# Fourteen matmuls with an unread result between the output projection's matmuls

## The chip, the cores and the metric

One core of a Trainium2 chip runs the kernel. The metric is the device time of one execution in microseconds (us); less is better. The number compared is the median of the runs shown. The engines are TensorE (PE in the profile, with its weight loads as PEld), VectorE (DVE), ScalarE (ACT), GpSimd (POOL) and SyncE (SP), which here issues most of the transfers.

## The reference

A gated sum of an attention decode step and a small MLP, for 8 batch rows with one token each. The keys and values used are the last 1024 positions of caches of 4096.

```python
x = A_x                                        # 8, 1, 448
g = sigmoid((x * gate_w).sum(-1, keepdims=True))
# attention: 16 query heads, 8 kv heads, head size 256, window W = 1024
q = (x @ wq) in heads
scores = einsum("bhqd,bhkd->bhqk", q, k[last W]) * 256 ** -0.5
o = einsum("bhqk,bhkd->bhqd", softmax(scores), v[last W])
a = o.reshape(8, 1, 4096) @ wo                 # 4096 x 448
# MLP
h = gelu(layernorm(x) @ w1 + b1)               # 1792 wide
b = h @ w2 + b2
return g * a + (1 - g) * b
```

## The kernel before

All 77.7 MB of inputs go through a ring of four large SBUF slots, in one order written out by hand: keys and values batch by batch, then the MLP weights (w12), the last values ("v", 7), and at the end the output weights wo. SyncE issues these loads; a slot is filled again when its reader has said done(). For each batch the kernel transposes keys, forms scores in the PSUM tile S_ps, takes the softmax, and multiplies by the values; the softmax and value steps of a batch lie between the key transposes of the next. The instruction order on each engine is the order of the program, since the schedule is manual.

After the last batch come the MLP's hidden layer (mlp_hidden, which gives hs) and the last values (L504, into PO, then oP). The output stage follows, from L628. It multiplies 46 chunks of 128 rows with their weights: 14 chunks of hs with w2, then 32 chunks of oP with wo, which are numbered 0 to 31 here. The first 34 of the 46 are wide: L640 adds each over 448 columns into one of four groups of 32 PSUM partitions of A1, so that four matmuls that follow each other use different columns of the PE array. VectorE then adds the four groups' tile and b2s into accs (L647). The last 12 chunks, 20 to 31, are narrow: L656 splits each into two halves of 224 columns, which go to the tiles A2[0] or A2[1] by the list part; accs itself is brought in by a matmul with pick at place EARLY = 4 among them, after chunk 23. When the last matmul into A2[1] is through, VectorE copies that tile to early (L664); after the last into A2[0] it adds both into res (L665), and two DMAs write res out (L667).

The output weights come in seven transfers (cuts, L166): chunks 0 to 7, 8 to 15, 16 to 19, 20 to 23, 24 and 25, 26 to 29, 30 and 31. TensorE waits for a transfer where it first needs one of its chunks. S_ps, the scores' tile, is last read by the exponential of batch 7 (L450); the identity tile ident is made at the start; the last value tile lies in its slot to the end.

Of the kernel before, what the change touches and what calls it, by code (L numbers as in the profile page):

```python
# [17 lines left out]
def kernel(  # L18
# [15 lines left out]
    nc = tc.nc  # L34
    P = nc.NUM_PARTITIONS

    NB, Sq, D = A_x.shape
    _, Hkv, Sk, Dh = A_k_cache.shape
# [16 lines left out]
    FB = FQ // BL  # L55
    HH = HD // 2
    FH = F // 2
    QN = 512
# [11 lines left out]
    TAIL = 12  # L70
    EARLY = 4
    DOUBLE = (4,)
    qscale = float(Dh) ** -0.5

    xf = A_x.rearrange("b s d -> (b s) d")
# [34 lines left out]
    def slot(*key):  # L110
        return slots[index[key]]
# [80 lines left out]
    ident = consts.tile([P, P], BF16)  # L192
# [4 lines left out]
    S_ps = ps_s.tile([P, W], F32)  # L197
# [149 lines left out]
    def transpose_keys(b, between=None):  # L347
        between = between or {}
        kn = slot("k", b)[:].bitcast(F32)
        for hh in range(NG):  # L350
            kt = ktpool.tile([P, QD, NCK, SK, NJ], BF16, tag="kt", name="kt")
            KT[hh] = kt
            for i in range(NCK // CB):
                g = hh * (NCK // CB) + i
                n = 2 if b in DOUBLE else 1
                if g < n:
# [278 lines left out]
        (hs[:, c, :], w2[:, OW2 + c * D : OW2 + (c + 1) * D]) for c in range(FB)  # L635
    ] + [(oP[:, c % J8, c // J8, :], w[:, c * D : (c + 1) * D]) for c in range(NCH)]
    wide, narrow = chunks[:-TAIL], chunks[-TAIL:]
    for i, (lhsT, rhs) in enumerate(wide):
        g = i % QD
        nc.tensor.matmul(  # L640
            A1[BL * g : BL * g + NB, :],
            lhsT=lhsT,
            rhs=rhs,
            start=(i < QD),
            stop=(i >= len(wide) - QD),
        )
    nc.vector.tensor_tensor(accs[:], A1[:], b2s[:], op=ALU.add)  # L647
    narrow.insert(EARLY, (pick[:], accs[:]))
    part = [1, 0, 1, 0, 0, 1, 1, 1, 0, 1, 0, 0, 0]
# [2 lines left out]
    for i, (lhsT, rhs) in enumerate(narrow):  # L652
        k = part[i]
        for h in range(2):
            g = 2 * k + h
            nc.tensor.matmul(  # L656
                A2[k][BL * g : BL * g + NB, :],
                lhsT=lhsT,
                rhs=rhs[:, h * DO : (h + 1) * DO],
                start=(k not in part[:i]),  # L660
                stop=(k not in part[i + 1 :]),
            )
        if 1 not in part[i + 1 :] and k == 1:
            nc.vector.tensor_copy(early[:], A2[1][2 * BL : P, :])  # L664
    nc.vector.tensor_tensor(res[:], A2[0][0 : 2 * BL, :], early[:], op=ALU.add)  # L665
# [32 lines left out]
```

## Time and profile before

| what | value |
|---|---|
| median of 3 runs | 190.55 us (190.50 to 190.69) |
| span of the profiled execution, first to last instruction | 188.9 us |
| PE busy / PEld busy | 118.8 us / 76.7 us |
| DVE / ACT / POOL busy | 111.7 / 90.6 / 59.0 us |
| mean granted TensorE clock | 0.876 |
| read from HBM | 77.67 MB, 411 GB/s over the span |
| last L504 matmuls start | 173.03 us |
| output stage's first matmul, L640 | 176.89 us |
| final addition L665 | 186.07 to 186.45 us |
| output DMAs issued, L667 | 186.48 us |

The page gives no total time for the profiled execution beside its span; the median of the runs is 1.65 us above that span. The granted clock is the share of full speed that the throttle allowed TensorE: 1.00 is full, 0.50 is half. A transfer's landing is seen as the moment at which an engine that waited for it goes on. Busy time of a matmul in the profile reaches to its modelled end, so it includes the time in which the result drains while the next matmul already streams.

### The profile page before, as it was taken

The page shows a single profiled execution, that of the slowest core. Times are in us where ns is not written, and L with a number is a line of the kernel's source. Part 1 is how long each engine was busy: PE and PEld are TensorE (multiplying, and loading weights), DVE is VectorE, ACT ScalarE, POOL GpSimd, SP SyncE. Part 2 cuts the span into 40 slices and gives each one's busy share as a digit, 9 for nine tenths or more (in the row PEclk, how much of TensorE's full clock was granted, in tenths as well). Part 3 has the DMA queues.
Part 4 walks back from the last instruction along what each step waited for, and adds up shares of the span by engine and source line. Part 5 has one row for each costly group of instructions (what it writes and reads, how often), then busy time and mean ns, then how long its engine had stood idle before and what let it go on. Part 6 is the DMA issues. An engine that isn't in the chain of part 4 may idle for free.

```text
span 188.9 us, 2891 instructions
## 1 busy us (share of the span) xinstructions
PE 118.8 (63%) x1100; PEld 76.7 (41%) x1100; DVE 111.7 (59%) x250; ACT 90.6 (48%) x102; POOL 59.0 (31%) x143
## 2 busy tenths in 40 slices
PE   0678609779775478846767478448853885273453
PEld 0656205555652176415642455147623772010110
DVE  4283783964789548716893487119821784947511
ACT  2298610894993239624762396218931884001000
POOL 8580000670670058003980391029201930000000
PEclk9996975999999969997899999858999799968555
DMA  5999999999999999999999999999999999999990
GB/s 203 418 427 425 451 420 425 434 437 427 420 435 431 434 423 430 428 437 430 420 437 434 434 420 430 437 423 432 423 437 427 434 423 424 418 425 438 413 389 34
DMA packets 7273, 77.86 MB, mean 412 GB/s; under 512 B 846, under 2 KB 1244, under 8 KB 2012
## 3 DMA queue, kind: packets, MB, share of 16 engines
q1 hardware_dynamic: 7226, 77.67, 96.9%
q8 instruction: 8, 0.13, 0.3%
q14 instruction: 5, 0.04, 0.1%
q10 hardware_dynamic: 34, 0.01, 0.0%
HBM read 77.67 MB, written 0.01 MB: 411 GB/s over the span
## 4 chain that ended last, share of the span: by engine, by line
DMA 75%; PE 9%; DVE 7%; ACT 6%; issue 1%; ACTq 0%; DVEq 0%
DMA slot<-in_A_k_cache_dram 45%; DMA slot<-in_A_v_cache_dram 14%; DMA slot<-in_A_wq_dram 8%; DMA slot<-in_A_wo_dram 8%; PE ktp L366 6%; ACT kt L372 5%; PE S_ps L433 2%; DVE kt L374 2%; DVE qw L425 1%; DVE qt L410 1%; DVE nmx L446 1%; DVE EB L457 1%; PE A L656 1%; DVE EZ L468 1%; PE S_ps L397 1%
## 5 line engine op out<-in xcount | busy, mean ns | idle before, releaser
L372 ACT COPY kt<-ktp 128x1024 bf16<-128x1024 bf16 x79 | 75.3, 1023 | 36.5 <-PE ktp L366 36.4
L366 PE MATMUL ktp<-ident_f,slot 128*128 128x128 f32 x476 | 72.0, 306 | 30.2 <-DMA slot<-in_A_k_cache_dram 21.2
L342 POOL COPY kt<-B 32x128 f32<-32x128 f32 (+1 forms) x128 | 54.9, 429 | 93.1 <-DVE B L334 88.1
L366 PEld LDWEIGHTS ktp<-ident_f,slot 128*128 128x128 f32 x476 | 59.6, 157 | 49.6 <-issue 23.4
L374 DVE COPY kt<-ktp 128x1024 bf16<-128x1024 bf16 x40 | 27.4, 685 | 15.1 <-PE ktp L366 14.8
L504 PE MATMUL PO<-slot,ET 128*16 128x512 bf16 x256 | 17.5, 417 | 15.1 <-DMA slot<-in_A_v_cache_dram 15.1
L450 ACT ACTIVATE E<-S_ps,nmx 128x1024 f32<-128x1024 f32 x8 | 8.9, 1114 | 30.3 <-DVE nmx L446 30.3
L334 DVE STREAM_TRANSPOSE B<-slot 128x512 f32<-128x512 f32 (+1 forms) x8 | 6.2, 778 | 28.4 <-DMA slot<-in_A_k_cache_dram 28.3
L433 PE MATMUL S_ps<-kt,qw 128*4 128x512 bf16 x256 | 17.8, 419 | 6.8 <-DVE qw L425 5.4
L504 PEld LDWEIGHTS <-ET 128*16 128x16 bf16 x256 | 6.4, 93 | 25.5 <-DMA slot<-in_A_v_cache_dram 11.3
L446 DVE TENSOR_REDUCE nmx<-S_ps 128x1 f32<-128x1024 f32 x8 | 9.8, 1222 | 10.1 <-PE S_ps L433 10.1
L433 PEld LDWEIGHTS <-qw 128*4 128x4 bf16 x256 | 6.6, 85 | 15.0 <-DVE qw L425 6.2
L457 DVE STREAM_TRANSPOSE EB<-E 128x1056 f32<-128x1056 f32 x8 | 10.2, 1269 | 1.3 <-ACT E L450 1.3
L530 DVE TENSOR_TENSOR oP<-Y 32x32 bf16<-32x32 f32 x32 | 10.3, 322 | 1.1
L487 DVE TENSOR_TENSOR ET<-sm,mask 128x512 bf16<-128x512 f32 x8 | 5.5, 692 | 2.2 <-PE sm L479 2.1
L517 DVE STREAM_TRANSPOSE T<-PO 128x512 f32<-128x512 f32 x8 | 5.7, 708 | 0.8 <-PE PO L504 0.7
L479 PE MATMUL sm<-EZ,perm 128*128 128x128 bf16 x8 | 1.7, 216 | 6.8 <-DVE EZ L468 6.8
L572 ACT ACTIVATE zb<-za 128x448 f32<-128x448 f32 x1 | 0.6, 576 | 10.7 <-DVE za L571 10.7
L522 DVE TENSOR_TENSOR Y<-T 64x64 f32<-64x64 f32 x16 | 4.8, 301 | 0.5
L468 DVE TENSOR_TENSOR EZ<-EB,sc 128x128 bf16<-128x128 f32 x8 | 4.0, 506 | 0.3
L640 PE MATMUL A<-slot,oP 128*8 128x448 bf16 x20 | 2.4, 551 | 1.8 <-DMA slot<-in_A_wo_dram 1.8
L425 DVE COPY qw<-qt 32x64 bf16<-32x64 bf16 x16 | 3.3, 206 | 0.3
(93 smaller groups left out, 53.7 us busy)
## 6 DMA issues: line engine op xcount, KB each, us to landing
slot<-in_A_k_cache_dram SPq DMA_DIRECT2D x14, 2048.0 KB, 28.1
slot<-in_A_v_cache_dram SPq DMA_DIRECT2D x14, 2048.0 KB, 33.9
slot<-in_A_k_cache_dram SPq DMA_DIRECT2D x4, 1024.0 KB, 8.0
slot<-in_A_v_cache_dram SPq DMA_DIRECT2D x4, 1024.0 KB, 24.5
slot<-in_A_wq_dram SPq DMA_DIRECT2D x3, 1024.0 KB, 12.5
slot<-in_A_wo_dram SPq DMA_DIRECT2D x2, 896.0 KB, 18.4
slot<-in_B_w_dram SPq DMA_DIRECT2D x1, 1568.0 KB
slot<-in_B_w_dram SPq DMA_DIRECT2D x1, 1344.0 KB, 26.5
```

Source lines behind the costliest of these rows:

```text
L334: nc.vector.transpose(B[:].rearrange("p c w s a -> p (c w s a)"), kn[:, 0 : n * P],)
L342: nc.gpsimd.tensor_copy(words[BL * w : BL * (w + 1), :, 0:n, g * S8 : (g + 1) * S8, 0], B[BL * g : BL * (g + 1), :, w].rearrange("p c s a ...
L366: nc.tensor.transpose(words[:, c, :, 0], kn[:, o : o + P], ident_f[:])
L372: nc.scalar.copy(dst, src)
L374: nc.vector.tensor_copy(dst, src)
L433: nc.tensor.matmul(S_ps[BL * t : BL * t + UR, n * QN : (n + 1) * QN], lhsT=qw[:, j, b, t, rep * u : rep * u + UR], rhs=KT[u][:, t, n * CQ ...
L446: nc.vector.reduce_max(nmx[:], S_ps[:], axis=AXIS.X, negate=True)
L450: nc.scalar.activation(E[:, 0:W], S_ps[:], ACT.Exp, bias=soft.pop(b)[:], scale=1.0, accum_out=E[:, W : W + 1],)
L457: nc.vector.transpose(EB[:].rearrange("p c r -> p (c r)"), E[:])
L468: nc.vector.tensor_tensor(EZ[:], EB[:, 0:NCK, 0:UR], sc[:].rearrange("p (o r) -> p o r", o=1).to_broadcast([P, NCK, UR]), op=ALU.mult,)
L504: nc.tensor.matmul(PO[BL * t : BL * t + Hq], lhsT=ET[:, c].rearrange("p u a r -> p (u a r)"), rhs=vn[:, c], start=(c < QD), stop=(c >= NCK ...
L530: nc.vector.tensor_tensor(oP[BL * i : BL * (i + 1), :, :, b], Yv[0:BL, :, :, i], Yv[BL : 2 * BL, :, :, i], op=ALU.add,)
```

## The change

A table FILL says after which chunk how many extra matmuls run. Its keys count chunks of oP from 0; -1 is the place after the last chunk of hs. In the wide loop the key is i - 14. In the narrow loop it is i + 20, where i also counts the place of accs: so 24 means after the accs matmul, 26 after chunk 25, and 30 after chunk 29. In all these are 2 + 4 + 2 + 2 + 1 + 2 + 1 = 14 matmuls. Each multiplies the 128x128 identity (bf16) with the first 512 columns of the last value tile and writes them to the first 512 columns of S_ps, which nothing reads afterwards.

```diff
     EARLY = 4
     DOUBLE = (4,)
+    FILL = {-1: 2, 7: 4, 15: 2, 19: 2, 24: 1, 26: 2, 30: 1}
...
     wide, narrow = chunks[:-TAIL], chunks[-TAIL:]
+
+    def run_on(n):
+        for _ in range(n):
+            nc.tensor.matmul(
+                S_ps[:, 0:QN],
+                lhsT=ident[:],
+                rhs=slot("v", NB - 1)[:, 0:QN],
+                start=True,
+                stop=True,
+            )
+
     for i, (lhsT, rhs) in enumerate(wide):
         g = i % QD
         nc.tensor.matmul(
...
             stop=(i >= len(wide) - QD),
         )
+        run_on(FILL.get(i - FB, 0))
     nc.vector.tensor_tensor(accs[:], A1[:], b2s[:], op=ALU.add)
...
                 stop=(k not in part[i + 1 :]),
             )
+        run_on(FILL.get(i + len(wide) - FB, 0))
         if 1 not in part[i + 1 :] and k == 1:
             nc.vector.tensor_copy(early[:], A2[1][2 * BL : P, :])
```

## The prediction

> **What bounds the kernel now.** I read the whole-span chain of waits first, then the chain of the last 29 us, then the timeline of the end, then busy time and granted clock in stretches of about 3.4 us. The page's chain by engine:
>
> ```profile
> DMA 75%; PE 9%; DVE 7%; ACT 6%; issue 1%; ACTq 0%; DVEq 0%
> ```
>
> Loading sets the span. Its end, in order of time (start us, length us, what):
>
> ```profile
> 170.56 14.32 DMA slot<-in_A_wo_dram
> 184.88 0.04 issue
> 184.93 0.54 PE A L656 x8
> 185.47 0.02 issue
> 185.49 0.56 PE A L656 x4
> 186.04 0.02 issue
> 186.07 0.38 DVE res L665
> ```
>
> The reader should see that nothing before 184.88 can save time by being faster: the output weights arrive then whatever TensorE does. Only 184.93 to 186.04, 1.11 us of TensorE, hangs on its speed. Now the timeline of the output stage (start, length, engine, line, what, count, idle before and its releaser):
>
> ```profile
> 176.89 1.66 PE L640 MATMUL A<-slot,hs 128*8 128x448 bf16 x14 [1.98 <-DVE oP L530]
> ...
> 178.94 0.92 PE L640 MATMUL A<-slot,oP 128*8 128x448 bf16 x8 [0.40 <-DMA slot<-in_A_wo_dram]
> ...
> 181.07 0.92 PE L640 MATMUL A<-slot,oP 128*8 128x448 bf16 x8 [1.21 <-DMA slot<-in_A_wo_dram]
> ...
> 182.17 0.54 PE L640 MATMUL A<-slot,oP 128*8 128x448 bf16 x4 [0.18 <-DMA slot<-in_A_wo_dram]
> ...
> 183.29 0.55 PE L656 MATMUL A<-slot,oP 128*8 128x224 bf16 x8 [0.58 <-DMA slot<-in_A_wo_dram]
> ...
> 184.93 1.10 PE L656 MATMUL A<-slot,oP 128*8 128x224 bf16 x12 [0.34 <-DMA slot<-in_A_wo_dram]
> 184.93 0.28 PEld L656 LDWEIGHTS <-oP 128*8 128x8 bf16 x8 [0.79 <-issue]
> 185.49 0.09 PEld L656 LDWEIGHTS <-oP 128*8 128x8 bf16 x3 [0.28 <-issue]
> ```
>
> TensorE stops before each piece of output weights. The last two lines matter most: the weight loads for chunks 30 and 31 start at 185.49, at the same moment as their matmuls, 0.28 us after the eight before them. The sets of matmuls before were 0.15 us apart (183.29, 183.44), so chunk 30 could have started near 185.25. It looks like every other start on a fresh piece. I read it as a sixth wait, for the last piece, which the chain cannot name because TensorE counts as busy draining; DMA traffic indeed ends only near 185.1. Last, busy time by stretch (length, then busy us of PE, PEld, DVE, ACT, POOL, then granted clock, DMA share, GB/s):
>
> ```profile
> 121.60:125.00 3.40, 1.53 (x19) 0.30 (x8) 0.00 (x0) 0.00 (x0) 0.00 (x0) 0.51 1.01 429
> 125.00:128.50 3.50, 3.00 (x14) 3.03 (x15) 1.67 (x3) 1.18 (x2) 1.97 (x6) 0.50 0.99 421
> 128.50:131.90 3.40, 2.73 (x22) 2.01 (x21) 2.99 (x8) 3.40 (x4) 3.11 (x8) 1.00 1.05 446
> ...
> 166.00:169.40 3.40, 3.25 (x26) 0.87 (x29) 1.09 (x3) 0.00 (x0) 0.00 (x0) 0.51 1.00 424
> 169.40:172.80 3.40, 0.47 (x8) 0.00 (x0) 2.62 (x6) 0.58 (x1) 0.00 (x0) 0.99 1.05 444
> ...
> 176.20:179.70 3.50, 2.41 (x22) 0.65 (x23) 1.66 (x6) 0.00 (x0) 0.00 (x0) 0.50 1.00 421
> 179.70:183.10 3.40, 1.62 (x16) 0.32 (x11) 0.34 (x1) 0.00 (x0) 0.00 (x0) 0.50 1.02 412
> ```
>
> Finely sampled, every change of clock falls on a grid of 3.41 us (15.83, 19.25, ... 169.46, 172.87, 176.28, 179.7, 183.1). A half-speed stretch with 2.96 us or more of busy TensorE is followed by full speed (125.0 above), one with 2.41 or less is not (176.2). A full-speed stretch stays so with 1.37 us and more, with one exception at 1.93, and falls with 1.06 or less. So the whole output stage now runs at clock 0.50.
>
> **The change, part by part.** It adds 14 matmuls and 14 weight loads on TensorE, no DMA, nothing on another engine; it moves and removes nothing. Inputs are old: the identity is from the start, the value tile has been read at 173.03, and S_ps was last read by the exponential, which ended at 160.08. So no filler waits for data; what waits is everything behind it on TensorE, and the addition of L647 behind the last L640 matmul.
>
> *Price of a filler.* No row has a 128-column stationary with 512 columns streamed. The two full-width L555 matmuls of 448 columns start 0.38 us apart at half clock (167.37, 167.75), 0.85 ns a column: 0.43 us for 512, and 0.215 at full clock, since 32 score matmuls take 3.82 us at half clock (28.51) and 1.99 at full (98.67). Its 128x128 bf16 weight load (row L479) takes 0.096 us at full and 0.15 at half. L555's loads of similar width cost no visible extra, so I take zero for the load, and 0.10/0.15 each as the upper end.
>
> *When the clock rises.* The 14 hidden-layer matmuls start at 176.89 and stream until 178.37 (four steps of 0.37, as 448-column sets do at half clock). Two fillers of 0.43 last to 179.24, which closes the 0.40 us gap; chunks 0 to 7 start 0.3 late and run on past the boundary at 179.7. The stretch then holds 2.76 us of busy TensorE, between 2.41 (no) and 2.96 (yes), nearer to yes. I take full clock from 179.7. The Trainium skill, TensorE: Matmul & The Clock Gate, Part 1, says that a busy window of about 3.4 us raises the clock and that the window runs free, unsynchronised with the kernel; the grid here agrees on 3.41 us, and one profile cannot show a phase that moves. Taken strictly (a wholly busy window), the rule would put the rise at 183.1, which is rival 2.
>
> *With full clock from 179.7:* chunk 7 streamed at 179.82; four fillers to 180.67; wait for 181.07; chunks 8 to 15 to 181.42; two fillers; chunks 16 to 19 from 182.15 to 182.34; two fillers to 182.76; chunks 20 to 23 from 183.27 to 183.46. The accumulated sum is ready earlier than before (matmul latency 0.35 for 0.54, then L647's 0.62), so its f32 matmuls, 0.37 instead of 0.75, end at 183.83; one filler to 184.04; chunks 24 and 25 and two fillers to 184.66, before 184.91. Chunks 26 to 29 stream to 185.10, the last filler to 185.31, still ahead of 185.47. All 14 fillers, 3.0 us at full price, thus lie in waits. Were that cover missing, the last one alone would cost 0.215.
>
> *What is won:* behind 185.47 stand chunks 30 and 31 on the same columns: a step of 0.187 and a latency of 0.37 = 0.56 now. At full clock the step is 0.093. The latency for 224 columns has no row; 128 columns take 0.216 (L479) and 512 take 0.380 (L504), which puts it at 0.257 on the line between. 0.35 against 0.56 is **0.21 us won**. DVE's copy early (0.39) ends at about 185.7, before the final addition at 185.86, so nothing takes the gain back. With the weight loads at their upper end the last filler ends at about 185.5, and 0.18 is won.
>
> The span goes from 188.9 to 188.7. The median shown, 190.55, is 1.65 above the span; that part lies outside the instructions and stays. **Forecast: 190.34 us.**
>
> **Rivals.**
>
> 1. *The last piece does not hold chunk 30*; what I read as its wait is TensorE's own. Then chunk 30 follows the last filler at 185.31: end at 185.66 for 186.04, and early's end at 185.70 limits it to 0.35 won: **190.20**. Against it is the 0.28 us gap and the simultaneous weight load; for it, that the chain names no DMA.
>
> 2. *The clock rises late and the fillers push the chain.* If 2.76 us is not enough, or the grid lies otherwise, fillers run at 0.43. Then four fillers end at 181.69 (0.6 after the piece landed), chunk 15 at 182.44, chunk 19 at 183.36, and L647's result at 184.25 against 183.38. The work still queued (f32 matmuls, a filler, chunks 24 and 25, two fillers) ends at 185.44 instead of before 184.91, the last filler at 185.84, the kernel 0.17 later: **190.72** with the rise at 183.1. The point from which it decides: a rise before 182.1 gives the forecast, 182.7 is even, 183.3 costs 0.47 (191.0). With exposed weight loads the rise at 183.1 would cost 1.2 (191.8). For it: before, that stretch stayed cold. Against: the fillers make TensorE busy without a pause, so a rise after 183.1 needs an unlucky phase.
>
> 3. *The clock stays at half.* By the same sum all fillers after 182.2 stand in the path: chunk 29 ends at 187.66, the last filler at 188.09, 2.6 lost: **193.15**. Continuous work has raised the clock in every such stretch of this trace (29.5, 67.0, 87.5, 145.5, 166.0), which speaks against it.
>
> 4. *Nothing shows*: the clock rises, but the last piece lands some 0.2 later, as transfers may from one program to another: **190.55**.
>
> **How the numbers follow.** Forecast 0.52, rival 1 0.14, rival 2 0.24, rival 3 0.05, rival 4 0.05. The bound of 0.2% (0.38 us), about what a measurement of this kernel can tell from no change, lies at 190.17 and 190.93. Faster: half of rival 1, and about a sixth of the forecast where landings come early: 0.16. Slower: rival 3 and a little over half of rival 2: 0.18. Within: 0.66. The forecast's own range is 190.15 to 190.55. The range to 8 in 10 goes down past rival 1 by the 0.15 that landings may scatter, to 190.05, and up through rival 2 with a rise as late as 183.3 to 191.1; it leaves out rival 3 and exposed weight loads.
>
> **What would show it.** Granted clock 1.00 from about 179.7 to the end; filler matmuls about 0.215 apart, the first two 0.43; chunk 30 still starting at about 185.5 relative to an unchanged last landing (rival 1: right behind its filler); its last matmul 0.35 after that start; L665 about 0.2 earlier. Wrong would be a clock of 0.50 beyond 182, DMA no longer releasing the matmuls of L640 and L656 but fillers running when the pieces land, fillers spaced by more than their columns, or an end of loading that differs by more than 0.2 us.

## The result and the profile after

The changed kernel takes 191.46 us in the median of 5 runs (191.25 to 191.79) against 190.55, a ratio of 1.0052 with a 95% interval of 1.0041 to 1.0063: slower, by about 0.9 us. Its profiled execution has a span of 189.5 us for 188.9. That is 0.6 of the 0.9: this run took 191.45 us, 1.95 above its span, and in the five runs this part outside the span is 1.76 to 2.35 us, against 1.73 to 1.85 in the 68 runs of the kernel before that stand beside the experiments below. What follows explains the longer span; no run shows what makes the other part.

First the page's chain of waits of the changed kernel, by engine:

```profile
DMA 67%; PE 17%; ACT 7%; DVE 6%; issue 2%; SPq 0%; ACTq 0%
```

TensorE's share went from 9% to 17%, and DMA's from 75% to 67%. The end of the chain, in order of time (start, length, what), shows where:

```profile
176.73 1.66 PE A L652 x14
178.39 0.54 PE S_ps L642
...
179.29 0.92 PE A L652 x8
180.21 1.82 PE S_ps L642 x4
...
186.34 0.38 PE A L669 x4
...
186.74 0.38 DVE res L679
```

L642 is the filler, L652 and L669 are the output matmuls that were L640 and L656, L679 is the final addition. No DMA stands in it from 176.73 to the end: the output weights no longer set the time, TensorE does, and L679 starts at 186.74 and not at 186.07, 0.67 us later. Now the timeline of the joints between fillers and chunks (start, length, engine, line, what, count, idle before):

```profile
179.29 0.92 PE L652 MATMUL A<-slot,oP 128*8 128x448 bf16 x8 [0.36 <-issue]
180.14 0.13 PEld L642 LDWEIGHTS <-ident 128*128 128x128 bf16 x2 [0.74 <-issue]
180.14 1.89 PE L642 MATMUL S_ps<-slot,ident 128*128 128x512 bf16 x4
...
181.96 0.10 PEld L652 LDWEIGHTS <-oP 128*8 128x8 bf16 x8 [0.84 <-issue]
...
185.72 0.37 PE L669 MATMUL A<-slot,oP 128*8 128x224 bf16 x8
186.01 0.10 PEld L642 LDWEIGHTS <-ident 128*128 128x128 bf16 x1 [0.19 <-issue]
...
186.33 0.09 PEld L669 LDWEIGHTS <-oP 128*8 128x8 bf16 x4 [0.23 <-issue]
```

Eight 448-column chunks from 179.29 stream for two steps of 0.37, to 180.04; the first filler comes at 180.14. Four fillers of 0.43 stream to 181.85; the next chunks come at 181.96. At full clock it is the same: two steps of 0.093 from 185.72 end at 185.91, the filler's load starts at 186.01 (its matmul has no row in the trace); its 0.215 would end at 186.22 if the matmul started with the load, and chunk 30 comes at 186.33. **Every change between the 128-column fillers and the 8-column chunks leaves about 0.10 us, in either direction and at either clock**, and weights that could be loaded ahead are not: their load starts only when the streaming has been over for that long (180.14 behind 180.04, 186.01 behind 185.91). Within the four fillers there is no such gap (1.89 is three steps of 0.43 and a last latency of 0.6). Seven groups make 14 changes, 1.4 us.

The clock, by stretches of the changed kernel (length, busy PE, PEld, DVE, ACT, POOL, then granted clock, DMA share, GB/s):

```profile
178.60:182.00 3.40, 3.04 (x17) 0.58 (x20) 0.00 (x0) 0.00 (x0) 0.00 (x0) 0.50 1.00 409
182.00:185.50 3.50, 3.50 (x36) 0.89 (x35) 0.62 (x1) 0.00 (x0) 0.00 (x0) 0.99 0.64 252
```

The fillers do raise it, at 182.04: the 3.41 us grid lies elsewhere in this execution than in the one before.

### The profile page after: what moved, and what is told of

It reads as the page before. It is cut to its first block, busy times and chain, and to the rows that moved or that the text cites. A ratio compares the mean times of both kernels' runs of the same rounds, so it can differ in the third digit from the quotient of the medians.

```text
span 189.5 us, 2917 instructions
## 1 busy us (share of the span) xinstructions
PE 123.5 (65%) x1112; PEld 77.8 (41%) x1114; DVE 111.4 (59%) x250; ACT 90.7 (48%) x102; POOL 59.2 (31%) x143
## 4 chain that ended last, share of the span: by engine, by line
DMA 67%; PE 17%; ACT 7%; DVE 6%; issue 2%; SPq 0%; ACTq 0%
DMA slot<-in_A_k_cache_dram 47%; DMA slot<-in_A_v_cache_dram 12%; DMA slot<-in_A_wq_dram 8%; PE ktp L367 8%; ACT kt L373 6%; PE S_ps L642 2%; PE S_ps L434 2%; PE A L652 2%; DVE qw L426 1%; DVE kt L375 1%; PE PO L505 1%; PE A L669 1%; DVE qt L411 1%; DVE nmx L447 1%; PE S_ps L398 1%
## 5 line engine op out<-in xcount | busy, mean ns | idle before, releaser
L367 PEld LDWEIGHTS ktp<-ident_f,slot 128*128 128x128 f32 x476 | 60.3, 158 | 48.7 <-issue 18.7
L505 PE MATMUL PO<-slot,ET 128*16 128x512 bf16 x256 | 18.8, 441 | 14.3 <-DMA slot<-in_A_v_cache_dram 14.3
L642 PE MATMUL S_ps<-slot,ident 128*128 128x512 bf16 x12 | 4.7, 484 | 0.0
L523 DVE TENSOR_TENSOR Y<-T 64x64 f32<-64x64 f32 x16 | 4.3, 268 | 0.6
L660 DVE TENSOR_TENSOR accs<-A,b2s 128x448 f32<-128x448 f32 x1 | 0.6, 625 | 5.4 <-PE A L652 5.4
```

Of the source, the lines that this page charges most:

```text
L367: nc.tensor.transpose(words[:, c, :, 0], kn[:, o : o + P], ident_f[:])
L505: nc.tensor.matmul(PO[BL * t : BL * t + Hq], lhsT=ET[:, c].rearrange("p u a r -> p (u a r)"), rhs=vn[:, c], start=(c < QD), stop=(c >= NCK ...
L642: nc.tensor.matmul(S_ps[:, 0:QN], lhsT=ident[:], rhs=slot("v", NB - 1)[:, 0:QN], start=True, stop=True,)
```

## The experiments

Theory 1: the loss is made of the changes of shape, together with the half clock up to the rise. Theory 2: it is the streaming of the fillers at half clock, whatever their shape. The ratios below are to the kernel before, run beside each version: its median was 190.58 us beside e1 to e4, and 190.50 beside e5 to e7 and the repeat.

**e1, fillers in the chunks' shape.** The same places and streamed columns, but each filler is four matmuls of 8 columns, one in each group of 32 partitions.

```diff
-                S_ps[:, 0:QN],
-                lhsT=ident[:],
+                S_ps[BL * g : BL * g + NB, 0:QN],      # g = 0, 1, 2, 3
+                lhsT=ident[:, 0:NB],
```

> Every filler becomes four matmuls of 8 identity columns, one into each group of 32 PSUM partitions, each streaming the same 512 columns: same streaming time, but in the same shape as the output matmuls around it. Theory 1 (each change between a 128-column filler and 8-column chunks costs 0.10 us, 14 of them, 1.4 us on a path with some 0.7 to spare): no gap of 0.10 us at the joints, and with a rise of the clock before 182.4 the time is 190.3 to 190.4; with a rise at 183.1, 190.7. Theory 2 (the time goes into the streaming of the fillers at half clock, whatever their shape): as after the change, 191.3 to 191.7.

Measured: 190.44, ratio 0.9994 (0.9986 to 1.0003). The chain of e1 has no idle time between chunks and fillers:

```profile
178.50 0.85 PE S_ps L642 x8
179.36 0.75 PE A L652 x8
180.10 1.71 PE S_ps L642 x16
181.81 0.66 PE A L652 x8
```

Its clock rose at 182.26, even later than after the change (182.04), and yet L679 starts at 185.88 against 186.74. As much was streamed at half clock, so theory 2 falls; 0.86 us go with the shape alone. Not all of them are gaps. After the matmul of accs, e1's first small fillers start at 183.83, beside the accs matmuls (183.81), which use two of the four groups; in the changed kernel the full-width filler at that place starts at 184.57, when the accs matmuls (184.09) have streamed.

**e2, the changes without the streaming.** Full-width fillers that stream 8 columns.

```diff
-                S_ps[:, 0:QN],
+                S_ps[:, 0:NB],
...
-                rhs=slot("v", NB - 1)[:, 0:QN],
+                rhs=slot("v", NB - 1)[:, 0:NB],
```

> The same 14 full-width fillers in the same places, but each streams 8 columns and not 512: the changes of shape stay, the streaming goes. The clock should stay at half to the end. Theory 1: by the sum at half clock the last weight load of chunk 30 comes at 185.76 and not at 185.47, so 0.28 us is lost: 190.8; gaps of about 0.10 us at every joint. Theory 2: 190.55.

Measured: 191.04, ratio 1.0033 (1.0018 to 1.0048), the clock at half to the end. The time is above the 190.8 expected. In its profile the piece with chunks 20 to 23 is seen 0.20 later than before (183.49 for 183.29), and from there TensorE is the chain. Two lines of its timeline are the filler after accs and chunks 24 and 25:

```profile
184.71 0.19 PE L642 MATMUL S_ps<-slot,ident 128*128 128x8 bf16 x1
184.83 0.54 PE L669 MATMUL A<-slot,oP 128*8 128x224 bf16 x4
```

Before chunk 26 two groups of short fillers cost 0.22 and 0.24. A further 0.37 goes because chunks 24 and 25 now stream behind the accs matmuls and the filler; in the kernel before they started at 183.86, beside the accs matmuls. Of these 0.83 us, 0.51 lie in time before chunk 26 in which nothing streamed in the kernel before (from about 184.41). The 0.32 left and the 0.20 make 0.52: chunk 26 starts at 185.45 for 184.93. The third group, 0.22 after chunk 29, lies but for 0.03 in the former wait for the last piece; L679 starts 0.55 later than before, at 186.62. Without any streaming worth the name the 14 fillers still make the kernel slower.

**e3, front fillers only.** Full width, but only the first six.

```diff
-    FILL = {-1: 2, 7: 4, 15: 2, 19: 2, 24: 1, 26: 2, 30: 1}
+    FILL = {-1: 2, 7: 4}
```

> Full-width fillers only after the last hidden chunk (2) and after chunk 7 (4). Theory 1: four changes of shape, 0.4 us, all before the 182.1 landing and covered; if the clock rises and stays, the two matmul steps behind the last landing fall from 0.56 to 0.35: 190.3 to 190.4. Theory 2 has the fillers after chunk 7 end 0.6 after their piece, and 0.5 us of waits left behind them: 190.3 to 190.6. If chunk 30 was never held by its landing, it starts right behind chunk 29 and 0.3 to 0.4 is won: 190.2.

Measured: 190.39, ratio 0.9995 (0.9986 to 1.0003). The end of its chain, and from its timeline the last matmuls:

```profile
173.00 12.45 DMA slot<-in_A_wo_dram
185.44 0.04 issue
185.48 0.38 PE A L669 x4
185.86 0.02 issue
185.88 0.38 DVE res L679
```

```profile
185.48 0.36 PE L669 MATMUL A<-slot,oP 128*8 128x224 bf16 x4 [0.18 <-DMA slot<-in_A_wo_dram]
```

At full clock TensorE is through with chunk 29 early, and now the trace names what chunk 30 waits for: the last piece, until 185.44. Behind it 0.38 us are left where there were 0.56. The gain that was hoped for is there, 0.18 to 0.19 us in the profile; in the times it is not clear of noise. In the spans it shows: nine of e3's eleven executions have 188.5 or 188.6 us, and none of the 35 of the kernel before beside them is under 188.7.

**e4, front fillers in the chunks' shape** (-1: 2, 7: 4, 15: 2, each as in e1).

> Fillers in the shape of the chunks, after the last hidden chunk (2), chunk 7 (4) and chunk 15 (2). Theory 1: no change of shape at all, full clock at the end: 190.3 to 190.4. Theory 2: between the front fillers alone and all of them, 190.4 to 191.0.

Measured: 190.41, ratio 0.9992 (0.9984 to 1.0001), L679 at 185.84. Of the versions tried it has the lowest ratio, but its interval just takes in 1, so that it beats the kernel before is not shown.

**e5, e6, e7: the price by itself.** e4 with short fillers between chunks 30 and 31, where nothing covers them. Theory 3, a rival within theory 1: only the uncovered load of 128 columns costs, and going back is free.

```diff
+        if i == len(narrow) - 2:
+            nc.tensor.matmul(                       # e5, and first in e7
+                S_ps[:, 0:NB], lhsT=ident[:],
+                rhs=slot("v", NB - 1)[:, 0:NB], start=True, stop=True)
+            for g in range(QD):                     # e6, and second in e7
+                nc.tensor.matmul(
+                    S_ps[BL * g : BL * g + NB, 0:NB], lhsT=ident[:, 0:NB],
+                    rhs=slot("v", NB - 1)[:, 0:NB], start=True, stop=True)
+            nc.tensor.matmul(                       # third in e7 alone
+                S_ps[:, 0:NB], lhsT=ident[:],
+                rhs=slot("v", NB - 1)[:, 0:NB], start=True, stop=True)
```

> Kernel e4 (fillers in the chunks' shape, only at the front; full clock at the end) with one full-width filler of 8 columns between chunks 30 and 31, where nothing covers it. Chunk 30 to the end of chunk 31 took 0.37 us in e4. Theory 1 (0.10 us for each change of shape): 0.20 more, 0.57; 190.6. Theory 3 (only the load of 128 identity columns is uncovered, going back is free): 0.10 more, 0.47; 190.5. If neither costs anything: 0.37 to 0.40, 190.4.

> As the one before, but the filler between chunks 30 and 31 is four matmuls of 8 identity columns and 8 streamed columns, in the chunks' shape. Theories 1 and 3: no change of shape, 0.37 to 0.45 us from chunk 30 to the end of chunk 31, 190.4. If any extra instruction there costs the same: as the one before.

> Between chunks 30 and 31: a full-width filler, the four in the chunks' shape, a full-width filler, each of 8 streamed columns. Theory 1: four changes, 0.40 us more than in e4, some 0.8 from chunk 30 to the end of chunk 31; 190.8. Theory 3: two loads, 0.20 more, 0.6; 190.6.

From the start of chunk 30 to the end of chunk 31 the profiles show 0.37 us in e4, 0.59 in e5 (0.22 more), 0.41 in e6 and 0.81 in e7 (0.44 more), in one profiled execution of each. Against e6, which adds matmuls but no change of shape, e5 has 0.18 more and e7 0.40. The medians are 190.52 for e5 (ratio 1.0000, 0.9991 to 1.0008), 190.43 for e6 (0.9993, 0.9984 to 1.0002) and 190.91 for e7 (1.0022, 1.0010 to 1.0033): against the kernel before only e7's loss is clear of noise in the times. The end of e7's chain:

```profile
185.39 0.26 PE A L669 x2
185.66 0.11 PE S_ps L678
185.77 0.11 PE S_ps L686 x4
185.88 0.11 PE S_ps L693
185.99 0.21 PE A L669 x2
```

L678 and L693 are the full-width fillers and L686 the four small ones between them. Each change adds 0.11 to the chain, also the one from the wide filler back to the small ones, so theory 3 falls.

**e8, e9: which width counts.** As e6, but with 64 identity columns in each half of the partitions (e8), or 32 in each group (e9).

> Kernel e4 with two fillers of 64 identity columns and 8 streamed columns between chunks 30 and 31, one into each half of the PSUM partitions. If any stationary wider than one group of 32 columns counts as another shape (theory 1): 0.20 us more between chunk 30 and the end of chunk 31, 0.57 to 0.60. If only the full 128 does: 0.37 to 0.42.

> Kernel e4 with four fillers of 32 identity columns and 8 streamed columns between chunks 30 and 31, one into each group of 32 PSUM partitions. If the shape is that of the group and not the 8 columns used (theory 1): no gap, 0.37 to 0.42 from chunk 30 to the end of chunk 31. If the number of columns loaded (32, not 8) counts: up to 0.2 more.

From chunk 30 to the end of chunk 31: 0.60 in e8, 0.40 in e9. A stationary of 64 columns changes the shape as 128 do; 32 columns in one group do not, though four times as many are loaded as the chunk's 8. Each of these two was run once.

**The changed kernel once more**, for another place of the grid.

> The changed kernel once more, for a second profile in which the 3.41 us grid of the clock may lie elsewhere. Theory 1 makes the loss depend on when the clock rises: nothing lost with a rise before 180.5, 0.4 us with 181.5, 0.7 with 182.0, 1.1 with 183.0, 1.3 with 183.5; L679 then starts that much after 186.07. If the loss did not come from half clock and changes of shape together, it would be 0.7 wherever the rise lies.

Measured: 190.94, ratio 1.0027 (1.0011 to 1.0044), so 0.4 us in the median where the first five runs gave 0.9. Single times go from 190.58 to 191.99, while e1 lay within 190.32 to 190.60. In this profile the clock rises at 179.92, and L679 starts only 0.03 after the kernel before:

```profile
186.10 0.38 DVE res L679
```

The sum of the prediction, done again with 0.10 for each change, gives 0.69 lost for a rise at 182.04 (0.67 measured) and 0.03 won for 179.92 (0.03 lost measured). Two profiles fix two points. The spans of these twelve executions, 188.7 to 190.0 us, fit the 0 to 1.3 us expected, but where the clock rose was not seen run by run. And the grid does not make the whole spread of the times: the profiled execution, with its early rise and a span of 188.9, took 191.69 us, 2.79 above its span. In the twelve runs this part outside the span is 1.74 to 2.79 us; its cause stays open.

## Why the prediction was wrong

It forecast 190.34 us and a range to 191.1; the kernel took 191.46.

*The bound.* Right. All that can be won lies behind the last landing, and the sixth wait, which was read from a weight load that started with its matmul, is named by e3's trace. Rival 1 falls.

*The gain.* Right in size where the fillers do not hold it back: 0.21 forecast, 0.18 to 0.19 in e3. In e1 L679 comes 0.19 earlier as well, though its chain names TensorE there and not the last landing. The latency for 224 columns at full clock, put at 0.257 between two rows, is 0.26 in e5.

*The rise of the clock.* The mechanism is right: a stretch of unbroken work raises the clock, and it stays to the end. The time was taken from the grid of one execution: 179.7 forecast, 182.04 in the profile after, 179.92 in the second, 182.26 in e1, 181.56 in e3 and 180.75 in e4. The Trainium skill's statement that the window runs free (TensorE: Matmul & The Clock Gate, Part 1) agrees with these five places. That 2.76 us of busy TensorE would be enough is not borne out. The stretches that raised the clock in these five held 3.05 to 3.42 us. In e2 the clock stayed at half behind a stretch with 2.73 us (176.63 to 180.05), and also behind one with 3.09 (183.46 to 186.87), while 2.97 raised it in e9. The profile's busy time counts draining, and e2's fillers stream little, so it is not the measure that decides; which one does stays open.

*The price of a filler.* **This is the step that failed:** "L555's loads of similar width cost no visible extra, so I take zero for the load". The pair of L555 matmuls, with 72 columns each, shows a wide matmul behind a wide one, and there it is indeed zero. What the change adds are wide matmuls between narrow ones. The trace before had that case, one line higher; from its timeline:

```profile
166.15 1.29 PE L544 MATMUL hp<-slot,xw 128*8 128x448 bf16 x12 [2.31 <-DVE hp L539]
167.37 0.96 PE L555 MATMUL hp<-slot,xw 128*72 128x448 bf16 x2
```

Twelve 8-column matmuls are three steps of 0.37 and end streaming at 167.27; the wide L555 starts at 167.37, 0.10 later. The Trainium skill has the rule as well: TensorEngine Tiling (Array Packing), Tiling Modes, Key Properties, says that changing the tiling mode, not just the tile, drains TensorE. The runs agree that a change costs and a new tile of the same mode does not (e6, e9), and add the price, 0.10 to 0.11 us each way. They may differ on how far the drain goes: in the changed kernel the load at 186.01 begins 0.10 after the chunks' streaming ends, and before their last results are out at 186.09, an end that the profile models.

*The sum.* "A rise before 182.1 gives the forecast" fell with it. Fourteen changes take 1.4 us. With the rise at 182.04 the four fillers at half clock and these gaps bring chunks 8 to 15 to 181.96 for 181.07, and from there each group adds two gaps to a queue that no longer waits for weights. So rival 2 came true in its mechanism, fillers pushing the chain, by gaps that I had priced at zero and, at its upper end, as exposed loads (191.8 with a rise at 183.1). The range left that end out. That the upper end comes near the loss is in part luck: it priced 14 loads, one for each filler, where the runs show 14 changes, and the loads of fillers that follow each other cost nothing (180.14 to 181.85 above).

*The part outside the span.* It was taken as 1.65 us, the median of the runs less the span of one profiled execution, and was to stay. In single runs of the kernel before it is 1.73 to 1.85, and in the 17 runs of the changed kernel 1.74 to 2.79. In the median of the first five it is about 0.1 more than before, which no step of the prediction had.

## What to carry to other kernels

Work put into a wait to keep the TensorE clock up must have the shape of the work around it: here a stationary that stays within one group of 32 partitions. Otherwise each visit costs a change in and a change out, and matmuls that ran side by side in different groups are forced one behind the other. Price an inserted instruction by a row in which it stands between the neighbours it will have, not between its own kind. And work meant to be hidden needs its slack counted at the slower clock and for any place of the clock's grid: in e3 the first six fillers alone raised the clock, and it stayed up to the end without those behind them.

## What the runs showed of the hardware

- Between stationaries of 8 or 32 columns in one group and those of 64 or 128, TensorE loses 0.10 to 0.11 us per change, in both directions, the same at granted clock 0.50 and 1.00 (e5 and e7 at full, e2 at half; 32 and 64 columns in one execution each, e9 and e8).
- In two profiles the same kernel ended 0.03 us late with a rise of the clock at 179.92 and 0.67 late with one at 182.04. Its times spread over 1.4 us (190.58 to 191.99), of which a part, up to 1 us in a single run, lay outside the span of its instructions.
